# Own PSUM tiles for the result banks, interleaved products, loads by four heads and norm steps on ScalarE, in a fused attention and feed-forward kernel

## The chip, the cores and the metric

The kernel runs on one core of a Trainium2 chip. In it TensorE (PE) multiplies and writes its results to PSUM; ScalarE (ACT) and VectorE (DVE) read PSUM; GpSimd (POOL) works in SBUF; SyncE (SP) issues most DMAs. The metric is the device time of a run in microseconds (us). A profile's "span" is about 2 us shorter than the time of the same run.

## The reference, cut to what matters

```python
# q, k, v: 8 batches x 12 heads x 448 x 64, float32;  tau = 0.1
q_n = q / (norm(q) + 1e-6);  k_n = k / (norm(k) + 1e-6)
attn = softmax(q_n @ k_n.T / tau);  x = attn @ v          # heads joined: 3584 x 768
h = x @ w_in                                              # 768 -> 2048, the "first product"
g = h * clip(h + 3, 0, 6) / 6
out = g @ w_out                                           # 2048 -> 768, the "second product"
```

## The kernel before

Heads are taken in pairs, 6 pairs a batch, 48 in all. A pair has four slots; each computes one block of scores, exponentiates it on ACT, and is filled with feed-forward matmuls of an earlier batch.

```python
X = [psum.tile([128, 2, 512], FP32, name=f"X{i}", tag=f"X{i}") for i in range(3)]   # 2 banks each
Y = psum.tile([128, 512], FP32, name="Y", tag="Y")
moe_banks = [X[2][:, 0, :], X[2][:, 1, :], Y[:, :]]       # X[0]: scores, X[1]: attn @ v

def mm1_unit(b, fc):                                      # one group of the first product
    ps = next_bank()                                      # the three banks in turn
    for cc in range(CC):                                  # 6 matmuls of 448 columns
        nc.tensor.matmul(ps[:, 0:S], w_in_sb[...], x[...], start=..., stop=...)
        ...
    nc.scalar.activation(out=u, in_=ps[:, 0:S], func=AF.Relu, bias=half_bias, scale=1/6)
    nc.vector.scalar_tensor_tensor(out=g[:, fc, ...], in0=u, scalar=1.0, in1=ps[:, 0:S], ...)
# mm2_unit: 16 matmuls of 384 columns, then a copy of ps by ACT or DVE in turn, then a store

def norms(i):                                             # 1 / (norm + eps) of a pair
    nc.vector.tensor_reduce(out=n2, in_=sq, ...)
    nc.scalar.activation(out=ln, in_=n2, func=AF.Ln)
    nc.scalar.activation(out=nr, in_=ln, func=AF.Exp, scale=0.5)
    nc.vector.tensor_scalar(out=ne, in0=nr, scalar1=EPS, op0=ALU.add)
    nc.vector.reciprocal(out=r, in_=ne)

for i in range(NP):                                       # 48 pairs
    if i % HP == 1 and i > HP:
        add_batch(i // HP - 1)                            # first, then second product of a batch
    for s in range(4):
        scores(i, s, ...)                                 # matmuls, then exp on ACT
        if s == 0:   ...  # load(i+4); square, normalise, cast on POOL; fill; rest of pair i-1
        elif s == 1: fill(0.8 * ns); back(i - 1); norms(i + 3); fill(0.2 * ns)
        elif s == 2: fill(0.4 * ns); transposes(i + 1); fill(0.6 * ns); values(i, 0); values(i, 1)
        else:        fill(ns); values(i, 2)
```

Each engine is given its instructions in this order of emission. All eight pieces of the weights are loaded before the loop.

## Time and profile before

| what | kernel before |
|---|---|
| time, median | 626.9 us |
| span of the profiled run | 624.0 us |
| PE busy, PE idle in the span | 468.8, 155.2 us |
| PE waiting for one of the three result banks | 99.1 us |
| first exp of pair 6; first matmul of the first product | 73.2; 79.0 us |
| from the first exp of the last pair to the end | 66.6 us |

The 99.1 us are five rows of the list of waits: PE at either product, waiting for gT or o (77.7, 9.4, 7.6, 3.9, 0.5). Busy PE time is not time at the peak: it counts the latency of the last matmul of every burst, about 0.16 us.

### The profile page before, as it was taken

To read this page: it belongs to the slowest core of one execution; us is meant where nothing else is said; L and a number is where in the kernel's file an instruction comes from. 1 tells how busy PE (TensorE), PEld (TensorE's weight loads), DVE (VectorE), ACT (ScalarE), POOL (GpSimd) and SP (SyncE) were. 2 spreads that over 40 slices of the span, in tenths; PEclk is the share of its full clock that TensorE was granted. 3 is DMA by queue.
4 is the path that set the end of the run, shared out by engine and by line. 5 is a ranking of instruction groups with operands and counts; after the bars stand their busy time and mean duration, and the time that the engine had idled before them with its cause. 6 is when DMAs were issued, how large, how long until landed. Compare 5 with 4: busy or idle time off the path is not lost.

```text
span 624.0 us, 9913 instructions
## 1 busy us (share of the span) xinstructions
PE 468.8 (75%) x3872; PEld 282.0 (45%) x3872; DVE 284.5 (46%) x667; ACT 260.4 (42%) x445; POOL 187.9 (30%) x154
## 2 busy tenths in 40 slices
PE   1464577796779976886779967798669887796786
PEld 0243344464445633553336644465336554463343
DVE  6552645436544455445442444435545365332310
ACT  1342555445543454344443434445444354433310
POOL 1742842234331432235221342216223332000000
PEclk9877799999999999999899989999999999999999
DMA  5999550035103351045101442025202340010012
GB/s 137 196 220 231 145 142 1 25 113 161 45 1 94 92 144 41 26 126 154 39 0 54 126 119 73 0 82 144 74 2 70 105 106 0 1 51 26 0 39 63
DMA packets 74158, 50.98 MB, mean 82 GB/s; under 512 B 24960, under 2 KB 74112, under 8 KB 74112
## 3 DMA queue, kind: packets, MB, share of 16 engines
q1 hardware_dynamic: 68864, 44.07, 25.7%
q0 software_dynamic: 5248, 6.29, 5.8%
q8 instruction: 30, 0.49, 0.3%
q14 instruction: 16, 0.13, 0.1%
HBM read 45.61 MB, written 11.01 MB: 91 GB/s over the span
## 4 chain that ended last, share of the span: by engine, by line
PE 54%; DVE 18%; ACT 12%; DMA 7%; issue 5%; SPq 3%; POOL 0%; DVEq 0%; ACTq 0%; POOLq 0%
PE X L267 15%; PE X L238 13%; DVE gT L251 7%; PE X L163 7%; PE Y L267 7%; DMA raw<-in_q_dram 7%; ACT u L248 6%; PE X L195 6%; DVE n L110 5%; PE Y L238 4%; ACT at L167 3%; DVE xT L222 2%; PE Z L221 1%; PE Z L133 1%; DVE o L281 1%
## 5 line engine op out<-in xcount | busy, mean ns | idle before, releaser
L167 ACT ACTIVATE at<-X 128x896 bf16<-128x896 f32 x192 | 156.6, 820 | 152.4 <-PE X L163 152.2
L238 PE MATMUL X<-xT,w_in_sb 128*128 128x448 bf16 x510 | 122.9, 356 | 78.3 <-DVE gT L251 77.7
L120 POOL TENSOR_TENSOR nrm<-raw,r 128x896 bf16<-128x896 f32 x46 | 77.8, 1691 | 225.6 <-DVE r L114 225.6
L238 PEld LDWEIGHTS <-w_in_sb 128*128 128x128 bf16 x768 | 72.9, 99 | 138.6 <-issue 86.3
L267 PE MATMUL X<-w_out_sb,gT 128*128 128x384 bf16 x608 | 118.5, 328 | 20.9 <-ACT o L279 9.4
L267 PEld LDWEIGHTS <-gT 128*128 128x128 bf16 x896 | 85.2, 98 | 78.6 <-issue 26.8
L163 PE MATMUL X<-qT,kz 128*128 128x448 bf16 x336 | 102.0, 376 | 17.8 <-ACT at L167 15.5
L101 POOL TENSOR_TENSOR sq<-raw 128x896 f32<-128x896 f32 x46 | 77.4, 1684 | 107.1 <-DMA raw<-in_q_dram 61.1
L251 DVE SCALAR_TENSOR_TENSOR gT<-u,X 128x448 bf16<-128x448 bf16 x85 | 52.7, 620 | 97.5 <-ACT u L248 96.5
L195 PE MATMUL X<-vx,at 128*128 128x65 bf16 (+1 forms) x1344 | 75.0, 204 | 19.7 <-ACT at L167 19.7
L195 PEld LDWEIGHTS <-at 128*128 128x128 bf16 x1344 | 66.9, 102 | 48.3 <-ACT at L167 22.1
L248 ACT ACTIVATE u<-X,half_bias 128x448 bf16<-128x448 f32 x85 | 53.6, 631 | 38.8 <-PE X L238 36.9
L111 ACT ACTIVATE ln<-n 128x14 f32<-128x14 f32 x48 | 10.3, 215 | 128.5 <-DVE n L110 128.5
L238 PE MATMUL Y<-xT,w_in_sb 128*128 128x448 bf16 x258 | 62.0, 359 | 0.0
L110 DVE TENSOR_REDUCE n<-sq 128x14 f32<-128x896 f32 x48 | 51.7, 1077 | 18.9 <-POOL sq L101 18.8
L267 PE MATMUL Y<-w_out_sb,gT 128*128 128x384 bf16 x288 | 56.1, 326 | 0.0
L163 PEld LDWEIGHTS <-kz 128*128 128x128 bf16 x336 | 31.0, 102 | 35.6 <-issue 19.6
L209 DVE RECIPROCAL rc<-X 128x8 f32<-128x8 f32 x48 | 9.8, 205 | 66.4 <-PE X L195 66.4
L133 PE MATMUL Z<-ident,nrm 128*128 128x128 bf16 x336 | 28.9, 231 | 10.2 <-DVE nrm L120 10.2
L222 DVE COPY xT<-Z 128x448 bf16<-128x448 bf16 x48 | 18.6, 388 | 34.8 <-PE Z L221 34.8
L251 DVE SCALAR_TENSOR_TENSOR gT<-u,Y 128x448 bf16<-128x448 bf16 x43 | 26.6, 619 | 16.2 <-ACT u L248 15.6
L210 DVE TENSOR_TENSOR on<-X,rc 128x512 bf16<-128x512 f32 x48 | 33.2, 691 | 1.7
(39 smaller groups left out, 258.4 us busy)
## 6 DMA issues: line engine op xcount, KB each, us to landing
raw<-in_q_dram SPq DMA_DIRECT2D x48, 192.0 KB, 2.8
raw<-in_k_dram SPq DMA_DIRECT2D x48, 192.0 KB, 2.8
vr<-in_v_dram SPq DMA_DIRECT2D x48, 192.0 KB, 2.8
out_dram<-o SPq DMA_DIRECT2D x48, 192.0 KB, 1.9
w_in_sb<-in_moe_w_in_dram POOLq DMA_DIRECT2D x4, 768.0 KB, 15.8
w_out_sb<-in_moe_w_out_dram POOLq DMA_DIRECT2D x4, 768.0 KB, 33.4
raw<-in_q_dram SPq DMA_DIRECT2D x48, 32.0 KB, 2.9
raw<-in_k_dram SPq DMA_DIRECT2D x48, 32.0 KB, 3.0
```

Of the source, the lines that this page charges most:

```text
L101: eng.tensor_tensor(out=sq[:, :, :], in0=a, in1=a, op=ALU.mult)
L110: nc.vector.tensor_reduce(out=n2[:, :], in_=sq[:, :, :], axis=AX.X, op=ALU.add)
L120: eng.tensor_tensor(out=nrm[:, :, :, :].rearrange("p s h d -> p h s d"), in0=raw_of[i][:, :, :, :], in1=r_of[i][:, :].rearrange("p (h s) - ...
L133: nc.tensor.transpose(Z[:, s * 128 : (s + 1) * 128], nrm[:, s, :, :], ident[:, :])
L163: nc.tensor.matmul(sc[:, n, 0:S], k_block(i, name), qT_of[i][:, :], start=True, stop=True)
L167: nc.scalar.activation(out=at[:, 0:m, :], in_=sc[:, 0:m, 0:S], func=AF.Exp, scale=inv_tau)
L195: nc.tensor.matmul(o, at[:, n, q_cols(i // HP, j)], mv, start=(name == "A0" and j % 2 == 0), stop=last, skip_group_check=True,)
L210: nc.vector.tensor_tensor(out=on[:, :, :, :].rearrange("p (b j) h d -> p b (j h) d", b=2), in0=pv4[:, :, :, 0:D], in1=rc[:, :, :].to_broad ...
L238: nc.tensor.matmul(ps[:, 0:S], w_in_sb[:, cc, fc * 128 : (fc + 1) * 128], x[:, cc, c0 : c0 + S], start=(cc == 0), stop=(cc == CC - 1),)
L248: nc.scalar.activation(out=u[:, :], in_=ps[:, 0:S], func=AF.Relu, bias=half_bias[:, :], scale=1.0 / 6.0)
L251: nc.vector.scalar_tensor_tensor(out=g[:, fc, c0 : c0 + S], in0=u[:, :], scalar=1.0, in1=ps[:, 0:S], op0=ALU.min, op1=ALU.mult,)
L267: nc.tensor.matmul(ps[:, 0:MH], lhs, w_out_sb[:, fc, m * MH : (m + 1) * MH], start=(fc == 0), stop=(fc == FCN - 1),)
```

## The change

It means to let PE go on while a result bank is emptied, to spread ACT's and DVE's feed-forward work evenly, to start sooner, and to relieve DVE.

```diff
-    X = [psum.tile([128, 2, 512], FP32, ...) for i in range(3)]
+    SC = psum.tile([128, 2, 512], FP32, ...); PV = psum.tile([128, 2, 512], FP32, ...)
-    moe_banks = [X[2][:, 0, :], X[2][:, 1, :], Y[:, :]]
+    moe_banks = [Y]
...                                    # from pair 6; until then a second score tile has the space
+            for n in range(2):
+                moe_banks.append(psum_m.tile([128, 512], FP32, name=f"M{n}", tag=f"M{n}"))
...                                    # weave: first product of b with the second of b - 1
+        first = [mm1_unit(b, fc) for fc in range(FCN)] if b < B else []
+        second = [mm2_unit(b - 1, t, m) ...]
+        for n, u in enumerate(first):
+            stream.append(u)
+            while second and ...: stream.append(second.pop(0))
...                                    # loads: two pairs at once, three buffers of two pairs
-        raw = sb.tile([128, 2, 7, D], FP32, name="raw", tag="raw", bufs=5)
+            raw_of[d] = sb.tile([128, 4, 7, D], FP32, name="raw", tag="raw", bufs=3)
...                                    # weights: one piece a pair instead of all at once
+                next_weights()
...                                    # norms: the last two steps from DVE to ACT
-        nc.vector.tensor_scalar(out=ne, in0=nr, scalar1=EPS, scalar2=None, op0=ALU.add)
-        nc.vector.reciprocal(out=r, in_=ne)
+        nc.scalar.activation(out=le, in_=nr, func=AF.Ln, bias=eps_bias)
+        nc.scalar.activation(out=r, in_=le, func=AF.Exp, scale=-1.0)
...
-        if i % HP == 1 and i > HP:
+            if i % HP == 0 and i > 0 and s == 2:
                 add_batch(i // HP - 1)
```

## The prediction

> **What bounds the kernel now.** I read the page first: no engine is busy for more than 75% of the span, and that one is the TensorE (PE), whose busy time also counts the latency of the last matmul of every group.
>
> ```profile
> PE 468.8 (75%) x3872; PEld 282.0 (45%) x3872; DVE 284.5 (46%) x667; ACT 260.4 (42%) x445; POOL 187.9 (30%) x154
> ```
>
> So I made a floor for PE from start-to-start times in the timeline: six 448-column matmuls in 1.13 us (0.1885 each), sixteen 384-column ones in 2.60 (0.1625), about 0.034 for one of 65 columns, 0.045 for 130, 0.056 for a transpose. Times the counts of the page: 768 and 336 at 0.1885, 896 at 0.1625, 1152 at 0.034, 192 at 0.045, 528 at 0.056 = **431 us**. 193 us of the 624 are lost. Next the waits say to what:
>
> ```profile
> PE X L238 <- DVE gT L251: 77.7, 57, 3.4
> PE X L267 <- ACT o L279: 9.4, 10, 2.3
> ```
>
> (us in total, times, longest.) The first feed-forward product (L238) waits 57 times for the VectorE (DVE) step that empties a result bank. The timeline of the last stretch, with no attention work left, shows why:
>
> ```profile
> 572.13 1.30 PE L238 MATMUL X<-xT,w_in_sb 128*128 128x448 bf16 x6 [1.38 <-DVE gT L251]
> 573.26 1.30 PE L238 MATMUL Y<-xT,w_in_sb 128*128 128x448 bf16 x6
> ...
> 574.80 1.30 PE L238 MATMUL X<-xT,w_in_sb 128*128 128x448 bf16 x6 [0.24 <-DVE gT L251]
> ...
> 576.14 0.63 ACT L248 ACTIVATE u<-X,half_bias 128x448 bf16<-128x448 f32 x1 [0.91 <-PE X L238]
> 576.80 0.62 DVE L251 SCALAR_TENSOR_TENSOR gT<-u,X 128x448 bf16<-128x448 bf16 x1 [0.92 <-ACT u L248]
> 577.48 1.29 PE L238 MATMUL X<-xT,w_in_sb 128*128 128x448 bf16 x6 [1.38 <-DVE gT L251]
> ```
>
> Three banks rotate, two of them halves of one tile X. The group at 577.48 goes into the half that was emptied long before, yet it starts only after the *other* half, filled from 574.80, has been emptied by ScalarE (ACT, 0.63) and DVE (0.62). Three groups take 577.48 - 572.13 = 5.35 us instead of 3 x 1.13 = 3.39. The wait is for the tile, not the bank. A count of matmuls by stretch, times the floor costs, gives floor over time: second product beside attention 29.7 of 32 us (0.93, from 183 us), first product beside attention 27.1 of 38 (0.71, from 215) and 26.3 of 43 (0.61, from 360).
>
> Last the start. Table by window: us, busy time of PE, PEld, DVE, ACT and POOL (GpSimd), granted clock, DMA share, GB/s; then two pieces of the chain that ended last:
>
> ```profile
> 20.00:40.00 20.00, 13.77 (x118) 9.30 (x117) 8.53 (x20) 7.67 (x13) 11.24 (x11) 0.75 1.19 212
> 40.00:60.00 20.00, 9.90 (x84) 5.70 (x83) 8.37 (x20) 7.01 (x12) 6.94 (x6) 0.76 1.16 220
> 60.00:80.00 20.00, 11.52 (x122) 7.39 (x120) 10.29 (x27) 9.55 (x17) 15.79 (x13) 0.81 0.63 163
> ```
> ```profile
> 36.08 13.22 DMA raw<-in_q_dram
> 49.31 12.51 DMA raw<-in_q_dram
> ```
>
> From 20 to 62 us the DMA engines are full: all eight weight pieces were queued at 16 to 22 us and share them with the q, k and v loads, so one pair of heads takes up to 11.6 us there (exp to exp), against 4.6 to 5.7 for pairs 5 and 6 just after. The first product starts at 79 us.
>
> **What the Trainium skill says.** "Perfetto Trace Analysis", Optimizing Tensor Performance: "Independent matmul groups should rotate through different PSUM banks so the ACT/DVE evacuation of one overlaps the next group's matmuls". The old kernel does so by address, and its trace shows that this was not enough. "PSUM — Partial Sum Buffer", PSUM bank collisions: the hazard is per bank and 32-partition quadrant, and accesses to different banks run clean; so nothing in the chip needs the wait above, and a tile for each bank may lose it. "TensorE: Matmul & The Clock Gate", Part 1: PE falls to half clock after an idle window of about 3.4 us; the trace agrees in kind, with 0.75 granted while PE starves from 20 to 60 us and 1.00 from 183. "ScalarE: Activation LUTs", Table sets: ln and exp share a set, so more of both costs no table load; the trace has one load of 1.28 us, with exp and ln alternating after it.
>
> **The change part by part.**
>
> *A tile for each bank.* Three separate one-bank tiles. In the built program each feed-forward group now waits for the emptying of the group three before it. Between them lie two groups, at least 2 x 1.13 = 2.26 us; emptying takes about 0.2 + 0.63 + 0.05 + 0.62 + 0.2 = 1.7. So the 77.7 us of waits and most of the smaller ones for o (9.4 and 3.9) should go, where PE is otherwise the bound.
>
> *Second product woven in.* Amounts stay: 768 + 896 matmuls. Each batch of attention (6 pairs, 18 us of floor at 3.0 a pair) now carries the first product of batch b (18.1) and the second of b-1 (15.6 or 20.8), evenly over its 24 slots, starting half a pair earlier. The batch from pair 6.5 to 12.5 has only the first product to carry. The end holds more: 18.1 + 15.6 + 20.8 = 54.5 us instead of 39, but without waits; the old end took 55.7 us from 568.3.
>
> *Loads by four heads, weights one piece per pair.* 7 issues per two pairs instead of 14; bytes unchanged, so a steady load costs the same. At the start three double loads (6 pairs) precede all weights but the first piece. Bytes until the load for pairs 8 and 9: 5 x 1.38 MB + 5 weight pieces x 0.79 (counted as written) = 10.8 MB, at 216 GB/s 50 us; the old kernel needed pairs 0 to 7 and all weights, 5.5 + 6.3 = 11.8 MB, by 62 us.
>
> *Norms on ACT.* 48 x (0.32 + 0.24) = 27 us leave DVE; 96 activations x 0.215 = 21 us come to ACT, and two engine crossings (25.4 us of DVE waiting for the norm) go. ACT per pair in a full batch: exp 3.28, norms 0.86, 2.67 u x 0.63 = 1.68, o 0.28 = 6.1 us of about 9.7. Off the path unless it delays an exp; I count zero.
>
> The sum: first exp at 16.5 us (19.1 now; faster issue from two queues), then 6.5 pairs at 7 us, DMA and latency together: first product at **62**. Batch 0: PE floor 6.0 us a pair, but the chain scores - exp - scores takes about 1.6 us for each of 3 slots and 1.0 for the last, 5.8, plus u and norms in the same ACT queue (2.5, part of it in the way): I take 7.3, so 44 us, to **106**. From pair 12.5 to 48 the program has 309 us of floor. The mm2 stretches reach 0.93; more ACT and DVE work lies between here, so I take 0.91: 340, to **446**. The rest is 66 us of floor at 0.97 = 68, and 4.5 for the last store: **519**, say 520.
>
> **Rivals.**
> *ACT takes over.* Its strict queue now holds four norm steps waiting for DVE's reduction (already 128.5 us of idle, 48 times) in front of an exp, beside u and o. For: exp gates the next scores, on a single score tile. Against: 6.1 of 9.7 us busy, and scores-to-exp needs 1.3 us in a slot of 2.4. If 1 us a pair is lost after pair 6, 40 us: about 560.
> *The start stays on DMA.* The same 19 MB have to come before batch 1, and a 4-head load lands later as a whole, with three buffers. For: 216 GB/s is the top seen. Against: only one weight piece competes at a time, and w_out is not needed before pair 12. If nothing is won at the start: about 535.
> *New tile waits from weaving.* The second product of b-1 reads the tile gT that the first product of b writes, for odd b. Waits on whole tiles would cost about 1.7 us at 6 places in 4 batches, some 40 us. Against: the waits in the built program lead to groups three back, by bank only. About 560 if I misread it.
> *PE floor reached.* 0.95 in the main part and 41 us in batch 0: about 500.
>
> **Range and chances.** My uncertain terms are start (+-6), batch 0 (+-5) and main part (0.88 to 0.95, +-13); put together some +-16 for one deviation, skewed to late by the rivals. Range 498 to 550. Faster by over 2% would fail only if two rivals cost 90 us together: 0.97, 0.02, 0.01.
>
> **What would show it right or wrong.** Right: PE's wait at the first product for gT falls from 77.7 to under 10 us; the end stretch has first-product groups 1.13 us apart; first product at 55 to 70 us; period of a pair in full batches 9.3 to 10.5 us all through, where it was 10 beside the second and 14 to 16 beside the first product; PE busy 80 to 88% of the span; DVE busy down by about 27 us, ACT up by 20. Wrong: scores waiting for exp for over 30 us (rival 1), a pair over 8 us before 60 us with DMA share above 1.1 (rival 2), PE waiting on gT at the second product (rival 3), or a granted clock below 0.95 after 100 us, which I assume away.

## The result, and the profile after

The changed kernel takes **511.9 us** (median of 4 runs, 509.5 to 512.6) against 626.9 (624.3 to 630.3): ratio 0.816, 95% interval 0.811 to 0.821. One of e2's four runs (633.0 us) is slow and left out of its ratio. Ratios are the mean time of one kernel's fast runs over that of the other's of the same rounds, so not quite the ratio of the medians. The forecast was 520, range 498 to 550.

The first row of the page after, engine busy times as before:

```profile
PE 449.6 (88%) x3872; PEld 274.9 (54%) x3872; DVE 259.3 (51%) x568; ACT 282.5 (55%) x543; POOL 189.3 (37%) x156
```

PE's idle time fell from 155.2 to 509.7 - 449.6 = 60.1 us, and its busy time by 19. Two things can do that, and no run separates them: in the traces PE's work falls into 65 stretches instead of 120, which at 0.16 us each is 9 us, and the mean granted clock is 0.990 instead of 0.967. DVE has 25 us less and ACT 22 us more. The longest waits of PE after the change (us in total, times, longest) show that no wait for a result bank is left, and what is:

```profile
PE SC L184 <- ACT at L188: 28.4, 36, 3.4
PE Z L154 <- DVE nrm L141: 11.4, 1, 11.4
PE PV L214 <- ACT at L188: 6.9, 5, 1.9
```

The timeline of the end (start, length, engine, line, operation) answers to the one shown in the prediction, where three groups took 5.35 us:

```profile
450.57 1.30 PE L257 MATMUL M<-xT,w_in_sb 128*128 128x448 bf16 x6
451.70 1.30 PE L257 MATMUL Y<-xT,w_in_sb 128*128 128x448 bf16 x6
...
452.84 1.30 PE L257 MATMUL M<-xT,w_in_sb 128*128 128x448 bf16 x6
453.98 2.76 PE L286 MATMUL M<-w_out_sb,gT 128*128 128x384 bf16 x16
```

Groups of the first product follow each other at 1.13 to 1.14 us, with no wait behind any of them. The start, in the table of windows (us, busy time of PE, PEld, DVE, ACT, POOL, granted clock, DMA share, GB/s):

```profile
20.00:40.00 20.00, 14.10 (x171) 9.03 (x168) 11.33 (x29) 13.96 (x30) 19.15 (x18) 0.91 1.19 224
40.00:60.00 20.00, 13.85 (x152) 8.60 (x151) 10.61 (x25) 13.25 (x27) 10.46 (x10) 0.91 1.15 233
60.00:80.00 20.00, 14.09 (x120) 8.01 (x119) 10.13 (x22) 10.35 (x22) 11.46 (x9) 0.91 0.79 180
```

The DMA engines are as full as before, yet ACT does 14.0 us of work from 20 to 40 us where it did 7.7: loads come in front of weights. The first product starts at 55.1 us instead of 79.0.

So far this looks like four parts that each did their work. The experiments say otherwise.

### The profile page after: what moved, and what is told of

Read it like the earlier page. It is cut to its first block, busy times and chain, and to the rows that moved or that the text cites. A ratio compares the mean times of both kernels' runs of the same rounds, so it can differ in the third digit from the quotient of the medians.

```text
span 509.7 us, 9679 instructions
## 1 busy us (share of the span) xinstructions
PE 449.6 (88%) x3872; PEld 274.9 (54%) x3872; DVE 259.3 (51%) x568; ACT 282.5 (55%) x543; POOL 189.3 (37%) x156
## 4 chain that ended last, share of the span: by engine, by line
PE 60%; ACT 15%; DVE 10%; DMA 7%; SPq 4%; issue 2%; POOL 1%; ACTq 0%; POOLq 0%
PE M L286 17%; PE M L257 13%; PE SC L184 9%; PE Y L286 8%; ACT at L188 7%; PE Y L257 7%; DVE n L129 6%; DMA raw<-in_q_dram 5%; PE PV L214 4%; ACT le L134 2%; DVE xT L241 2%; PE Z L240 2%; SPq L95 1%; ACT u L267 1%; ACT nr L133 1%
## 5 line engine op out<-in xcount | busy, mean ns | idle before, releaser
L188 ACT ACTIVATE at<-SC 128x896 bf16<-128x896 f32 x192 | 156.4, 820 | 65.2 <-PE SC L184 63.7
L184 PE MATMUL SC<-qT,kz 128*128 128x448 bf16 x336 | 97.9, 363 | 29.7 <-ACT at L188 28.4
L257 PE MATMUL M<-xT,w_in_sb 128*128 128x448 bf16 x510 | 120.8, 353 | 0.0
L286 PE MATMUL M<-w_out_sb,gT 128*128 128x384 bf16 x608 | 118.1, 326 | 0.0
L286 PEld LDWEIGHTS <-gT 128*128 128x128 bf16 x896 | 84.5, 98 | 60.2 <-issue 5.2
L257 PEld LDWEIGHTS <-w_in_sb 128*128 128x128 bf16 x768 | 72.5, 98 | 77.3 <-issue 22.1
L270 DVE SCALAR_TENSOR_TENSOR gT<-u,M 128x448 bf16<-128x448 bf16 x85 | 52.7, 621 | 98.3 <-ACT u L267 97.9
L214 PEld LDWEIGHTS <-at 128*128 128x128 bf16 x1344 | 64.0, 99 | 30.8 <-ACT at L188 9.3
L214 PE MATMUL PV<-vx,at 128*128 128x65 bf16 (+1 forms) x1344 | 71.7, 199 | 7.0 <-ACT at L188 6.9
L267 ACT ACTIVATE u<-M,half_bias 128x448 bf16<-128x448 f32 x85 | 53.4, 630 | 22.6 <-PE M L257 22.3
L257 PE MATMUL Y<-xT,w_in_sb 128*128 128x448 bf16 x258 | 63.1, 355 | 0.0
L286 PE MATMUL Y<-w_out_sb,gT 128*128 128x384 bf16 x288 | 56.7, 326 | 0.0
L154 PEld LDWEIGHTS <-nrm 128*128 128x128 bf16 x336 | 23.9, 101 | 23.5 <-DVE nrm L141 11.4
L229 DVE TENSOR_TENSOR on<-PV,rc 128x512 bf16<-128x512 f32 x48 | 33.2, 691 | 1.7
## 6 DMA issues: line engine op xcount, KB each, us to landing
w_in_sb<-in_moe_w_in_dram POOLq DMA_DIRECT2D x4, 768.0 KB, 11.7
```

Source lines behind the costliest of these rows:

```text
L154: nc.tensor.transpose(Z[:, s * 128 : (s + 1) * 128], nrm[:, s, :, :], ident[:, :])
L184: nc.tensor.matmul(sc[:, n, 0:S], k_block(i, name), qT_of[i][:, :], start=True, stop=True)
L188: nc.scalar.activation(out=at[:, 0:m, :], in_=sc[:, 0:m, 0:S], func=AF.Exp, scale=inv_tau)
L214: nc.tensor.matmul(o, at[:, n, q_cols(i // HP, j)], mv, start=(name == "A0" and j % 2 == 0), stop=last, skip_group_check=True,)
L229: nc.vector.tensor_tensor(out=on[:, :, :, :].rearrange("p (b j) h d -> p b (j h) d", b=2), in0=pv4[:, :, :, 0:D], in1=rc[:, :, :].to_broad ...
L257: nc.tensor.matmul(ps[:, 0:S], w_in_sb[:, cc, fc * 128 : (fc + 1) * 128], x[:, cc, c0 : c0 + S], start=(cc == 0), stop=(cc == CC - 1),)
```

## The experiments

My theory, from the waits before: the tile that two banks shared is most of the gain, and the other parts give the rest. The rivals: the weaving hides the emptying; the start; the norms.

### One part alone, and one part undone

**e1, own tiles alone.** The kernel before, with this edit only:

```diff
-    X = [... for i in range(3)];  moe_banks = [X[2][:, 0, :], X[2][:, 1, :], Y[:, :]]
+    X = [... for i in range(2)];  moe_banks = [M0, M1, Y]      # three tiles
...                                                            # as in the change, the second score tile of the start has the space until pair 6
```

> The kernel before with one edit: the three feed-forward result banks are three tiles, order of work, loads and norms as they were. My theory (the wait for the shared tile is most of the gain): PE's wait for gT at the first product falls from 77.7 us to under 10, the last stretch takes about 44 us instead of 55.7, and the time falls to 540 to 560 us. Rival (the weaving is what hides the evacuation, the banks alone only move the wait to exp or to the score tile): 590 us or more, with the scores waiting for exp.

Measured: 514.8 us, ratio 0.819 (0.816 to 0.822), better than I expected, and not to be told apart from the whole change (0.811 to 0.821). PE waits for no result bank any more; its longest waits are old ones for exp:

```profile
PE X L195 <- ACT at L167: 20.4, 6, 6.9
PE X L163 <- ACT at L167: 19.3, 32, 6.2
```

**e2, the changed kernel without own tiles.**

```diff
-                moe_banks.append(psum_m.tile([128, 512], FP32, ...))
+            MM = psum_m.tile([128, 2, 512], FP32, name="MM", tag="MM")
+                moe_banks.append(MM[:, n, :])
```

> The changed kernel with one edit undone: two of the three result banks are again halves of one tile. My theory: the wait for gT returns, with 60 to 90 us in total over 184 groups, and the time is 570 to 600 us. Rival (with the products woven there is enough work between two groups to hide the evacuation): under 530 us.

Measured: 628.1 us (median of four, the slow run with them), ratio 0.997 of the fast runs (0.991 to 1.003): the kernel before, to within the error. PE's waits at the two products (L257, L286) are back:

```profile
PE MM L257 <- DVE gT L270: 51.5, 29, 3.7
PE MM L286 <- DVE gT L270: 32.2, 22, 3.9
...
PE MM L257 <- ACT o L298: 13.5, 11, 2.8
```

With three small rows not shown, 6.6, 0.6 and 0.6 us, they make 105 us, against 99.1 before. So the weaving hides nothing of the emptying, and the rival falls. Both runs together: **own tiles are worth all of the 115 us, and the other three parts, as they stand together, nothing.** That they did nothing was not expected. The start alone was 21 us shorter (first exp of pair 6 at 52.7 in e2 and 52.2 after, 73.7 in e1). The question is where those 21 us went.

The first exp of pair 6 and of pair 47, read off the timelines, split each span in three:

| span | to pair 6 | pair 6 to 47 | pair 47 to the end |
|---|---|---|---|
| e1, own tiles alone, 512.9 us | 73.7 | 386.5 | 52.7 |
| the whole change, 509.7 us | 52.2 | 387.4 | 70.1 |

The change defers the second product, so 18 us more of matmuls are left for the end (66 us of PE floor from the first scores of pair 47 on against 48, matmuls counted in the traces, at the prediction's costs). The middle has 18 us less to do and takes as long. The loss is in the middle.

### Which part loses

**e3, old order.** The changed kernel with both products of a batch one after the other, spread as before from pair 7.

> The changed kernel with the old order of the feed-forward work: both products of a batch one after the other, spread evenly over all that is left, from pair 7. If weaving is what keeps ACT and DVE evenly loaded, pairs beside the first product rise to 11 us or more and the time is 520 to 540 us. Rival (with own tiles the order no longer matters, and the old order leaves 39 instead of 54 us of floor for the end and fills pairs 7 to 12 with 10 us of matmuls each): 500 to 510 us.

Measured: 516.9 us, ratio 0.821 (0.818 to 0.825). Most pairs beside the first product took 10.4 to 11.3 us (pair 13 took 12.5, pair 7 13.6), yet not even the low end of the first theory's time was reached: the weaving is worth about 1% (the intervals overlap a little), and the rival's 500 to 510 is wrong as well.

**e4, norms back on DVE.**

```diff
-        nc.scalar.activation(out=le, in_=nr, func=AF.Ln, bias=eps_bias)
-        nc.scalar.activation(out=r, in_=le, func=AF.Exp, scale=-1.0)
+        nc.vector.tensor_scalar(out=ne, in0=nr, scalar1=EPS, scalar2=None, op0=ALU.add)
+        nc.vector.reciprocal(out=r, in_=ne)
```

> The changed kernel with the last two norm steps back on DVE. The prediction counted zero for them: 507 to 517 us, with DVE busy up by 27 us and ACT down by 25. Rival (the norm steps on ACT delay exp, or the two crossings matter): a difference of over 5 us, up or down.

Measured: **493.4 us**, ratio 0.784 (0.781 to 0.788). I had counted zero; moving two small steps to the less loaded engine had cost 18.5 us, 4%. The timeline shows how. First pair 28 of the changed kernel:

```profile
262.64 0.54 PE L184 MATMUL SC<-qT,kz 128*128 128x448 bf16 x2
262.77 1.08 DVE L129 TENSOR_REDUCE n<-sq 128x14 f32<-128x896 f32 x1
...
263.88 0.22 ACT L132 ACTIVATE ln<-n 128x14 f32<-128x14 f32 x1 [1.78 <-DVE n L129]
...
264.77 0.21 ACT L135 ACTIVATE r<-le 128x14 f32<-128x14 f32 x1
264.89 0.90 ACT L188 ACTIVATE at<-SC 128x896 bf16<-128x896 f32 x1
...
265.84 0.35 PE L184 MATMUL SC<-qT,kz 128*128 128x448 bf16 x1 [0.34 <-ACT at L188]
```

The scores of the third slot are done at 263.18, and ACT is idle. But the norm steps stand before the exp in ACT's queue, and they wait for DVE's reduction. The exp starts at 264.89, 1.7 us after its data, and the next scores find the score tile occupied. The same place in e4:

```profile
253.34 0.54 PE L184 MATMUL SC<-qT,kz 128*128 128x448 bf16 x2
253.47 1.08 DVE L129 TENSOR_REDUCE n<-sq 128x14 f32<-128x896 f32 x1
...
254.94 0.90 ACT L188 ACTIVATE at<-SC 128x896 bf16<-128x896 f32 x1
...
256.04 0.35 PE L184 MATMUL SC<-qT,kz 128*128 128x448 bf16 x1
```

With two steps fewer in front, the exp starts 1.06 us after its data, and the scores behind it wait for nothing. Two windows over the same program part, from pair 12.5 to the first scores of pair 47, give the sum: first after the change, then in e4 (columns as in the table of windows above):

```profile
111.00:438.90 327.90, 314.18 (x2783) 195.03 (x2781) 179.53 (x387) 199.44 (x383) 124.79 (x97) 1.00 0.30 83
...
110.00:421.80 311.80, 311.02 (x2783) 194.32 (x2781) 190.94 (x453) 183.56 (x317) 124.94 (x97) 1.00 0.31 88
```

PE hardly rests in e4. Of the 18 us between the two kernels, 16 come from this stretch.

**e6, old order and norms on DVE**, so the kernel before plus own tiles plus new start and loads:

> e3 (old order of the feed-forward work) with the norms back on DVE as in e4; so this is the kernel before plus own tiles plus the new start and loads. If the weaving is worth something once the norms are out of the way, this is slower than e4's 493 us by over 5; if the order does not matter, 488 to 498. The start alone should give 20 us against e1's 514.8, as pair 6 begins at 53 instead of 74 us: 490 to 497.

Measured: 497.3 us, ratio 0.792 (0.787 to 0.797). The start is worth 17.5 us against e1. Against e4 the old order is 4 us, 1%, slower, and the two intervals overlap a little; with e3 in the same direction I take the weaving as worth about 1%, no more, though neither pair alone shows it clear of noise.

The tally, in medians: own tiles 627 to 515; start and loads to 497; weaving to 493; norms on ACT back to 512.

### Is it the place or the amount of the norm steps?

**e5, the whole norm chain earlier in its slot.**

```diff
             elif s == 1:
+                if i + 3 < NP:
+                    norms(i + 3)
                 fill(0.8 * ns); back(i - 1)
-                if i + 3 < NP:
-                    norms(i + 3)
```

> The changed kernel with one call moved: the norm steps of a slot are put ahead of the matmuls that fill it, so that DVE's reduction no longer stands behind the copy of the attention result. The four ACT steps stay. Theory 1 (e4 was faster because the longer norm chain, starting late behind DVE's reduction, holds up the exp behind it in ACT's queue): the chain starts right after the exp before it, exp is no longer late, and the time comes near e4's, 490 to 500 us. Theory 2 (it is the mere 25 us more of ACT work that costs): 507 us or more.

Measured: 509.9 us, ratio 0.814 (0.810 to 0.818): by time, theory 2. Its profile tells something else. PE's longest waits but for the one at the start:

```profile
PE Z L154 <- DVE xT L241: 26.0, 15, 5.0
...
PE SC L184 <- ACT at L188: 7.6, 6, 4.4
```

The wait for exp fell from 28.4 to 7.6 us, and pairs 13 to 18 run at 8.1 to 9.0 us, much as in e4 (8.4 to 9.1). But now DVE's reduction stands in front of the copy xT, and where the squares are late (pairs 5 to 9 took up to 14.1 us) DVE holds up the transposes; the granted clock was low there too, 0.82 from 70 to 110 us. One queue's wait had become another's. e5 did not settle the question.

**e9, only the ACT steps moved, behind the last exp of the pair.** The reduction stays.

```diff
-                    norms(i + 3)                 # slot 1
+                    sums(i + 3)                  # slot 1: the reduction
             else:
+                if i + 3 < NP:
+                    roots(i + 3)                 # slot 3: ln, nr, le, r
                 fill(ns); values(i, 2)
```

> The changed kernel with the four ACT norm steps moved behind the last exp of the pair; DVE's reduction stays where it was. If e4's gain came from the place of the chain in ACT's queue (in front of the third exp, waiting for the reduction), then the same four steps cost nothing here: batches 1 to 6 at 9.0 us a pair as in e4, batch 0 at 7 us a pair instead of 8.7, and 480 to 495 us. If the amount of ACT work costs, 505 to 512.

Measured: **485.0 us**, ratio 0.772 (0.768 to 0.777), with all four steps on ACT. In the same program part PE is busy without a break:

```profile
108.00:418.00 310.00, 310.00 (x2777) 194.12 (x2775) 179.54 (x387) 200.02 (x380) 123.83 (x97) 1.00 0.32 89
```

ACT is busy 200.0 us there, as after the change (199.4). So in the full batches the amount of ACT work costs nothing; its place in the queue cost it all. There, that is settled.

It explains a part of batch 0 as well (pairs 6.5 to 12.5, with only the first product to carry), which took 8.5 to 9.6 us a pair, pair 7's 11.7 apart, for about 6 of PE floor. The chain that ended last in the changed kernel, start and length:

```profile
81.98 0.92 ACT at L188
82.89 0.53 ACT u L267
...
83.45 0.62 DVE gT L270
84.07 0.30 DVE xT L241
84.37 1.00 DVE n L129
...
86.51 0.81 ACT at L188
...
87.36 0.35 PE SC L184
```

(the four norm steps are left out before 86.51). Hardly a link from the second exp on is needed by the next exp's data: it is the order of two queues, ACT's and DVE's. In e9 pairs 8 to 11 take 7.2 to 7.9 us, so more than 1 us a pair over the floor stays unexplained.

### The start, and the stall after it

**e7, all weights issued at once, loads by four heads kept.**

> The changed kernel with all eight weight pieces issued at once before the first pair, the four-head loads kept. If spreading the weights is what made the start short, pairs 2 to 5 take 8 to 12 us again and pair 6 begins at 65 to 75 instead of 52 us, time 520 to 530. If the larger loads and their lead of six pairs did it, pair 6 stays below 58 us and the time within 5 us of 512.

Measured: 514.2 us, ratio 0.820 (0.816 to 0.824). Pair 6 begins at 59.4 us, between the two cases. So of the 21 us by which the start is shorter than in e1, spreading the weights gives 7 and the rest of the new start 14; the larger loads and their longer lead are the likely reason, but no run takes them alone. But pair 7 takes 8.7 us in e7 and 11.7 after the change, so only about 2 us of the spreading reach the end.

**e8, w_out at pairs 8 to 11.** The stall behind that: GpSimd waits for a load while w_out is under way. After the change, its longest wait from 52 to 68 us:

```profile
POOL sq L119 <- DMA raw<-in_q_dram: 8.0, 1, 8.0
```

> The changed kernel with the four pieces of w_out issued at pairs 8 to 11 instead of 3 to 6. GpSimd waited 8 us at 56 to 64 us for the load of pairs 10 and 11, which stood behind weights; the second product is not needed before pair 13. If that stall is on the path, pair 7 to 8 falls from 11.7 to 8 or 9 us and the time by 3 to 6 us, 506 to 509. If batch 0 is bound by its own chain anyway, within 2 us of 512.

Measured: 508.6 us, ratio 0.812 (0.808 to 0.816), inside the expected 506 to 509, but with an interval that overlaps the change's, so the gain of 3 us is not clear of noise. Pair 7 fell to 8.7 us as expected, and in the profiled run, the slowest of the four, pair 6 rose from 6.9 to 9.3. No load explains that rise: the one wait of the squares for v, 7.8 us, lies at 6 to 14 us. What differs is the granted clock: it was 0.50 from 54.2 to 61 us, where it was 1.00 in pair 6 after the change, and PE was busy for 7.8 us with that pair's work instead of 5.1. What the order of these loads is worth stays unresolved.

### Versions that beat both

**e10**: e9, the last two norm steps on DVE, w_out late.

> e9 with the last two norm steps on DVE as in e4 and w_out issued late as in e8. e4 and e9 remove the same wait, so their gains do not add up; against e9 only e8's 1 to 3 us and a little of ACT's queue are left: 478 to 492 us. If it is slower than e9, the DVE queue has taken the place of ACT's.

Measured: 479.8 us, ratio 0.764 (0.760 to 0.769). That is 5.2 us less than e9. The profiled spans are 3.0 us apart, nearly all of it before pair 13. Two things changed, so it isn't shown whether the smaller amount of ACT work in batch 0 or the late w_out did it.

**e11**: e10 with half of each batch's second product in its own batch, w_out from pair 6.

> e10 with half of each batch's second product moved from the next batch into its own, w_out from pair 6: batch 0 carries 8 us more of matmuls, the end 8 us less. If the slots of batch 0 have room (floor 6 us a pair against 7 or more measured), 3 to 8 us faster than e10; if the new groups wait for gT, which has only just been written, or for w_out, no gain.

Measured: **475.1 us**, ratio 0.757 (0.752 to 0.762). All outputs were correct. Batch 0, now with 8 us more work, takes 6.5 to 8.4 us a pair. The best of these kernels is thus 37 us faster than the change as it was made.

## Why the prediction was right or wrong, point by point

- **The bound and its cause: right.** The shared tile was the cause; waits for result banks went from 99.1 us to none, not just "under 10", and e1 and e2 show it alone and by its absence. In e1 the span fell by 111.1 us: idle by 95.5 and busy by 15.6.
- **The sum: right by terms that cancel.** Predicted against the span: first product at 62, measured 55.1; batch 0 44, measured 56; the main part 340, measured 328; the rest 72.5, measured 70.8. That the total came within 9 us is in part luck. A granted clock of 1.00 from 111 us on, assumed there, came too. (What the text calls pair 48 is the first score of pair 47: its 309 us of floor end there, and the 66 that follow begin there. The sum is not touched.)
- **The start: mis-sized by 7 us.** I took 7 us a pair from bytes over rate; the pairs took 5.0 to 6.9. Two readings of the old trace were off as well: 216 GB/s is not "the top seen" (the text's own table has 220, the page 231), and pairs 5 and 6 took 5.4 and 6.1 us by their first exps, not 4.6 to 5.7. The bytes came due later, at 56 to 64 us, as the stall before pair 8. Rival 2 was there, behind the place where I looked.
- **Batch 0: mis-sized by 12 us.** I added "part of" u and norms to the chain of exps. The chain also ran through DVE (gT, xT, reduction) by the order of its queue, and the load stall made pair 7 3 us longer than in e7.
- **Norms on ACT, "I count zero": the step that failed.** It cost 18.5 us (e4), and with all four steps behind the last exp (e9) the same kernel is 27 us faster. I had named the mechanism in rival 1, a queue in which norm steps wait ahead of an exp, and argued it away with a busy share, 6.1 of 9.7 us. (The two steps took 0.31 and 0.21 us a pair, 25 us in all and not 21; that is not where the loss came from.) A busy share says nothing about what stands in front of what. My sign for it, over 30 us of scores waiting for exp, stayed just unreached at 28.4 and was too coarse: 13.6 of them fell in the main part, where the norms cost 16 us.
- **Main part at 0.91: 0.94 measured**, and it would have been 0.99 with the norms on DVE. I had explained the expected loss with the amount of ACT and DVE work; e9 shows that the amount costs nothing there. Also, the old 0.61 from 360 us was not all waits: the granted clock was 0.92 in that stretch, so "1.00 from 183" did not hold throughout.
- **Weaving and the start as sources of gain: not borne out for the kernel as changed.** Each gave what it could (1%, 17.5 us), and the norms gave as much back.
- **Rival 3, waits on gT: rightly dismissed.** No such wait appears after the change.

## What to carry to other kernels

Two buffers that are to be filled and emptied in turn must be separate for whatever makes the waits, here the tile; look at what a wait names, and whether the buffer it protects is the one that is waited for. An instruction that moves to a less busy engine goes into a queue: ask what it will wait for there and what stands behind it. Two steps of 0.2 to 0.3 us a pair, in front of an exp, cost 18.5 us in all (e4), and behind the last exp all four cost nothing in the full batches (e9). When a change has several parts, time each alone: here one part gave everything, the start helped, the weaving by 1% at most, and the norms took back what they gave.

## What the Trainium skill lacked or had wrong

- "TensorE: Matmul & The Clock Gate", Back-to-back issue gap, gives about 81 ns a matmul at 128 columns and 131 at 512 for streams of weight load and matmul. Here, with a load for every matmul, 448 columns take 188 ns start to start (six in 1.13 us) and a 128-column transpose 56 ns (seven in 0.39); the page's formula for the isolated gap fits both within 2 ns.
- "ScalarE: Activation LUTs", What ACT_TABLE_LOAD costs, speaks of a cost for every switch to a different set. The changed kernel asks a second time for the set that it has, and the trace shows a full second load of 1.28 us at 6.25 us.
- No page has it: a wait can be for the whole tile although its banks are apart, worth 114 us here (e1 against the kernel before, same rounds).
- No page gives a size for what an instruction that waits in ACT's queue costs a ready one behind it: 27 us here (the change against e9).
